# One order of 2925 operations replaced by another in a fused recurrence and MLP kernel

## The chip, the cores and the metric

The kernel runs on one core of a Trainium2 chip. The metric is the time of one execution on the device in microseconds (us); less is better. The engines are named PE (TensorE, the matrix engine, with its weight loads as PEld), DVE (VectorE), ACT (ScalarE), POOL (GpSimd) and SP, whose queue issues nearly all transfers. Each engine works through its own instructions in order; semaphores hold one until what it needs from another engine or a transfer is there.

## The reference

For 4 x 8 heads, 768 steps and head width 40, a recurrence on a 40 x 40 state reads `y = r . state`, decays the state by `w`, subtracts the product of `state . a` with `b` and adds that of `v` with `k`. All heads' `y`, laid side by side to 320 numbers per token (3072 tokens), go through a gated MLP without a nonlinearity. `moe_w1` to `moe_w_out` come as 64-bit floats, the rest as 32-bit.

```python
def _attn_ref(r, k, v, w, a, b):
    for t in range(S):
        y[:, :, t] = np.einsum('bhd,bhde->bhe', rt, state)
        Sa = np.einsum('bhde,bhe->bhd', state, at)
        state_decay = state * wt[:, :, None, :] - np.einsum('bhd,bhe->bhde', Sa, bt)
        state = state_decay + np.einsum('bhd,bhe->bhde', vt, kt)
...
def _moe_ref(x, w1, w2, w3, w_out):
    a = x @ w1
    b = x @ w2
    h = a * b @ w3
    return (h @ w_out).astype(np.float32)
```

## The kernel before

**Stages.** The 768 steps are cut into 12 chunks of 64. For each chunk, the four batches are taken in two pairs. A pair is loaded (`load`: ld.fm, ld.xx, ld.aa), scaled by the running product of `w` (`scale`: sc.max, sc.scan, sc.ln, sc.exp, sc.aa, sc.gt, sc.gi, sc.xs), and multiplied into the triangular blocks of the chunk (`causal`: ca.mm and its copies and masks). `solve` inverts these blocks on DVE (so.in, then some 35 small operations so.x, so.td, so.tt), and `join` puts the parts together on PE. `pairs` and `tokens` (pa, tk) prepare further operands. `rec` then applies them for the two batches of a pair at a time: r.zv, r.s, r.zn, r.t0, r.t1, r.t2, r.tr, all matmuls of line 870; between r.t0 and r.t1, and between r.t1 and r.t2, DVE makes one masked product `un` each (r.u, line 921). With two pairs in a chunk there are 24 in all. `gather` moves the results of a chunk by twelve small transfers (ga, line 946), and `mlp` runs the MLP of the chunk: m.xh and m.xl split the input in two, m.mm1 are the wide matmuls (line 987), m.a, m.ab, m.gh and m.gl their results, m.mm2 (line 1012) the second product, m.o and m.out the output.

**Weights.** Ahead of all this, `weights` reads the 31 blocks of 64-bit weights (cv.in, 512 KB each) into four buffers `raw` and makes 32-bit numbers of them (cv.t and cv.add on DVE, cv.r on ACT, cv.sign on either), and `product` multiplies the last two weight matrices on PE (w3.mm, line 539). The MLP can't begin before this is done (the last `nil`). At the end `proof` reads the blocks a second time (ck.in) and checks their range (ck.abs, ck.sq, ck.max).

**The order.** Every operation is declared by `op` with its kind, what it reads and what it writes. `Order.place` (line 300) sorts all of them by `RANK[kind][n]`, where n counts the operations of a kind in the order of their declaration; the ranks are a permutation of 0 to 2924. It hands out buffers in that order (`SLOTS`, line 35: 4 raw, 3 xx, 3 aa, 4 fm, 8 banks of PSUM, one y and one xr), emits the instructions in it, and ties every instruction to the one before it on its engine. So RANK fixes the order on each engine and in SP's queue, and semaphores do the rest:

```python
placed, done = sorted(self.ops, key=lambda o: RANK[o["kind"]][o["i"]]), set()
```

**The choice of engine.** Seven kinds can run on two engines. `ON[kind]` has a letter for each of their operations: d for DVE, p for POOL, a for ACT (`both`). A POOL operation that shares its port with DVE is made to wait for the DVE operation of two inputs that stands last before it in the order (line 1143 on).

Of the kernel before, what the change touches and what calls it, by code (L numbers as in the profile page):

```python
# [55 lines left out]
    "cv.sign": "dddadaaaddddaaaadaaaaaaddaaaaaa",  # L56
    "cv.add": "dddddddddddddddddddppdpdpdpdddd",
    "w.lo": "ddppdpdddddp",
    "sc.aa": "ddddddddpdpppppppdppddpd",
    "sc.xs": "ddddddpppdddddpdddpdpdpd",  # L60
    "m.gl": "dddpdpddpppppppppdpppppdddpppppddppdpppdpddddddp",
    "ck.sq": "dddaaddadaaaaadddadaaaddaadadda",
}
RANK = {kind: [int(n) for n in ranks.split()] for kind, ranks in {
# [1198 lines left out]
```

## Time and profile before

| | before |
|---|---|
| runs, us | 604.8, 596.65, 604.96 |
| median of the runs, us | 604.8 |
| profiled execution, us | 607.17 |
| its span, first to last instruction, us | 605.5 |
| mean granted clock of PE, share of full speed | 0.976 |
| instructions | 26713 |

The profile is of one execution with a time of its own, 607.17 us, of which its 605.5 us of span are recorded; busy times, waits and clocks are of that execution, while the median is over the runs. Busy shares are means over stages with different limits. A wait is put down to the semaphore that came last; "issue" is idle time for which the profile shows no releaser.

### The profile page before, as it was taken

Reading aid. Unit: us, or ns where it says so; the run is one execution under the profiler, and the core shown is the slowest. Engines: PE = TensorE matmul, PEld = TensorE weight load, DVE = VectorE, ACT = ScalarE, POOL = GpSimd, SP = SyncE. Lnnn points to the kernel's source line nnn. Section 1 sums busy time; section 2 is a strip of 40 time slices with the busy share of each in tenths; the row PEclk is TensorE's granted clock in tenths of the full one; section 3 lists DMA queues with packets and bytes.
Section 4 is the critical chain, followed back from the end, with each engine's and each line's share of the span. In section 5 each row is a group of like instructions: output and inputs, shape, how many; then the busy total and the mean of one; then the engine's idle time right before and its main releaser. Section 6 shows DMA issues by size and latency. Waiting matters only on the chain.

```text
span 605.5 us, 26713 instructions
## 1 busy us (share of the span) xinstructions
PE 546.8 (90%) x11714; PEld 490.9 (81%) x11714; DVE 494.3 (82%) x950; ACT 414.2 (68%) x889; POOL 156.3 (26%) x222
## 2 busy tenths in 40 slices
PE   1298988899999799999999899998999999999994
PEld 1276666799988799898898799898898989988994
DVE  6999879999599777795797797995998978956663
ACT  6878949855847647648756649649578488477762
POOL 3012332122412312244323223044141142031000
PEclk9997989899999979999999999999999999999998
DMA  8997875350244335223353343532665343255681
GB/s 254 308 289 232 267 202 162 72 160 15 75 114 117 83 91 139 64 68 99 100 127 109 90 116 104 136 85 64 162 168 146 105 129 110 93 157 180 210 253 59
DMA packets 56812, 83.45 MB, mean 138 GB/s; under 512 B 30320, under 2 KB 38000, under 8 KB 56688
## 3 DMA queue, kind: packets, MB, share of 16 engines
q1 hardware_dynamic: 56300, 81.34, 47.4%
q8 instruction: 94, 1.54, 1.1%
q10 hardware_dynamic: 388, 0.33, 0.2%
q14 instruction: 30, 0.25, 0.1%
HBM read 72.99 MB, written 3.93 MB: 127 GB/s over the span
## 4 chain that ended last, share of the span: by engine, by line
PE 47%; DVE 17%; ACT 16%; DMA 8%; issue 5%; SPq 4%; POOL 1%; ACTq 0%; DVEq 0%; POOLq 0%
PE bank L987 19%; PE bank L870 12%; PE bank L1012 5%; ACT JP L329 4%; ACT TT L329 4%; PE bank L539 3%; SPq L946 3%; DVE tmp L680 3%; PE bank L628 2%; PE bank L845 2%; DMA raw<-in_wo_dram 2%; DMA raw<-in_w3t_dram 2%; PE bank L821 1%; DVE TDX L656 1%; DVE un L921 1%
## 5 line engine op out<-in xcount | busy, mean ns | idle before, releaser
L987 PE MATMUL bank<-xs,W 128*128 128x256 f32 x1536 | 209.0, 288 | 0.0
L987 PEld LDWEIGHTS bank<-xs,W 128*128 128x128 f32 x1536 | 190.1, 191 | 7.3 <-issue 0.8
L830 POOL TENSOR_SCALAR_AFFINE_SELECT vg<-vg 64x256 f32<-64x256 f32 x96 | 40.3, 426 | 145.9 <-DVE tmp L680 72.2
L1003 POOL TENSOR_TENSOR gl<-ga,gh 128x512 fp32r<-128x512 f32 x28 | 36.1, 1290 | 121.7 <-DVE tmp L680 46.1
L1012 PE MATMUL bank<-W3h,gh 128*128 128x320 f32 x192 | 62.3, 324 | 0.2
L1012 PE MATMUL bank<-W3h,gl 128*128 128x320 f32 x192 | 59.6, 310 | 0.9 <-POOL gl L1003 0.5
L1012 PE MATMUL bank<-W3l,gh 128*128 128x320 f32 x192 | 59.2, 309 | 0.0
L870 PE MATMUL bank<-un,bk 64*40 64x104 f32 (+1 forms) x768 | 44.8, 255 | 10.0 <-DVE un L921 7.8
L644 POOL TENSOR_SCALAR_AFFINE_SELECT lm<-lm 64x512 f32<-64x512 f32 x48 | 33.5, 699 | 76.2 <-DVE tmp L680 25.4
L329 ACT ACTIVATE JP<-bank 64x256 f32<-64x256 f32 (+2 forms) x120 | 45.2, 378 | 10.8 <-PE bank L628 8.3
L329 ACT ACTIVATE ga<-bank 128x512 f32<-128x512 f32 x48 | 28.6, 598 | 30.8 <-PE bank L987 30.5
L870 PE MATMUL bank<-hs,TT 64*64 64x104 f32 x768 | 46.6, 260 | 2.2 <-ACT TT L329 1.7
L329 ACT ACTIVATE gh<-ga 128x512 fp32r<-128x512 f32 x48 | 30.2, 631 | 25.5 <-DVE ga L1000 24.2
L870 PEld LDWEIGHTS bank<-un,bk 64*40 64x40 f32 (+1 forms) x768 | 35.7, 124 | 13.6 <-DVE un L921 11.2
L921 DVE TENSOR_TENSOR un<-bank,mask_h 128x416 f32<-128x416 f32 x48 | 28.1, 584 | 22.7 <-PE bank L870 22.6
L870 PE MATMUL bank<-vg,bk 64*40 64x104 f32 (+1 forms) x768 | 45.0, 255 | 0.3 <-issue 0.2
L1000 DVE TENSOR_TENSOR ga<-bank,ga 128x512 f32<-128x512 f32 x48 | 32.8, 686 | 13.1 <-ACT ga L329 7.2
L870 PEld LDWEIGHTS bank<-hs,TT 64*64 64x64 f32 x768 | 36.7, 136 | 7.5 <-ACT TT L329 3.0
L539 PE MATMUL bank<-wof,w3f 128*128 128x320 f32 x128 | 42.7, 488 | 0.0
L628 PE MATMUL bank<-aa,xx 40*64 40x64 f32 x1536 | 30.5, 232 | 12.9 <-DVE xx L600 5.5
L628 PEld LDWEIGHTS bank<-aa,xx 40*64 40x64 f32 x1536 | 27.4, 145 | 17.3 <-issue 8.7
L680 DVE TENSOR_TENSOR tmp<-Tp,TDX 128x256 f32<-128x256 f32 (+2 forms) x57 | 39.9, 700 | 1.0
(126 smaller groups left out, 1265.5 us busy)
## 6 DMA issues: line engine op xcount, KB each, us to landing
rv<-in_rv_dram SPq DMA_DIRECT2D x24, 588.0 KB
xx<-in_fmx_dram SPq DMA_DIRECT2D x24, 448.0 KB
raw<-in_w3t_dram SPq DMA_DIRECT2D x16, 512.0 KB
JP<-in_w3t_dram SPq DMA_DIRECT2D x11, 512.0 KB
fm<-in_fmg_dram SPq DMA_DIRECT2D x24, 227.5 KB
aa<-in_fma_dram SPq DMA_DIRECT2D x24, 224.0 KB
raw<-in_w_dram SPq DMA_DIRECT2D x10, 512.0 KB
vg<-in_vt_dram SPq DMA_DIRECT2D x48, 80.0 KB
```

What stands on the lines that cost most here:

```text
L329: act.activation(out_, in_, AF.Copy, scale=scale)
L539: pe.matmul(out=pt.t[:, 0:DM], lhsT=w[:, j], rhs=wof[:, j], start=(j == 0), stop=(j == NJ - 1))
L628: pe.matmul(out=bank(s)[64 * z:64 * z + 64, i, p], lhsT=X[r, p, z], rhs=aa.t[r, i, p], start=True, stop=True)
L644: op("ca.mask", lambda q=q: pool.affine_select(out=lm.t[q], in_=lm.t[q], pattern=[[0, 2 * NP], [1, C]], compare_op=ALU.is_gt, fill=0.0, ba ...
L680: dve.tensor_tensor(out=scratch(*shape), in0=x().to_broadcast([128, *shape]), in1=y().to_broadcast([128, *shape]), op=ALU.mult)
L830: op("pa.mask", lambda q=q, vg=vg: pool.affine_select(out=vg.t[q, :, 0:C], in_=vg.t[q, :, 0:C], pattern=[[0, NP], [1, C]], compare_op=ALU. ...
L870: pe.matmul(out=out_(ab ^ z, p), lhsT=left(ab, ab ^ x, p), rhs=right(ab ^ x, p), start=start and p == 0, stop=True, skip_group_check=True)
L921: dve.tensor_tensor(out=un[i].t, in0=view(hp[i]), in1=mask_h.unsqueeze(1).to_broadcast([128, NP, N]), op=ALU.mult)
L987: pe.matmul(out=pt.t[:, TOK * x:TOK * x + TOK], lhsT=WT[k][:, cs], rhs=xs.t[:, z], start=(n == 0), stop=(n == 7))
L1000: op("m.ab", lambda a=a, pt=pt: dve.tensor_tensor(out=a.t, in0=wide(pt), in1=a.t, op=ALU.mult), r=[pt], w=[a])
L1003: both("m.gl", lambda e, a=a, j=j: e.tensor_tensor(out=gl.t[:, j:j + 2], in0=a.t, in1=gh.t[:, j:j + 2], op=ALU.subtract), r=[a, (gh, j)], ...
L1012: pe.matmul(out=pt.t[:, 0:DM], lhsT=l.t[:, j, ts], rhs=W3[r][:, j], start=(j == 0 and n == 0), stop=(j == NJ - 1 and n == 2))
```

## The change

The two tables ON and RANK get other numbers. Each kind has as many operations as before, no instruction's shape or count changes but for the engine that runs it, and the rest of the file is the same. All 79 kinds have other ranks. In ON, cv.sign has 22 letters a instead of 20 (of 31), cv.add 5 p as before at other places, w.lo 3 p instead of 4, sc.aa 9 instead of 11, sc.xs 4 instead of 7, m.gl 30 instead of 28 (and its last letter is d instead of p), and ck.sq 13 a instead of 16. The order is described as made anew for the same structure, with later landings assumed for the first transfers. Of the diff, all of ON and the kinds that are spoken of:

```diff
--- before.py
+++ after.py
@@ -53,199 +53,200 @@
 ON = {
-    "cv.sign": "dddadaaaddddaaaadaaaaaaddaaaaaa",
-    "cv.add": "dddddddddddddddddddppdpdpdpdddd",
-    "w.lo": "ddppdpdddddp",
-    "sc.aa": "ddddddddpdpppppppdppddpd",
-    "sc.xs": "ddddddpppdddddpdddpdpdpd",
-    "m.gl": "dddpdpddpppppppppdpppppdddpppppddppdpppdpddddddp",
-    "ck.sq": "dddaaddadaaaaadddadaaaddaadadda",
+    "cv.sign": "aadaaddaadadaaaaddaaaaaadaadaaa",
+    "cv.add": "dddddddpdddddddddddpdpddddpdpdd",
+    "w.lo": "dddpddpddddp",
+    "sc.aa": "ddddddddpdpppddppdpdpdpd",
+    "sc.xs": "ddddddpddddddppdddpddddd",
+    "m.gl": "ddddppppppdpdpdpdpppddpppdpdpppdpppdpppppppdddpd",
+    "ck.sq": "ddaaaaaaddddaddadddaadaadddddda",
 }
...
-    "z.bk": "10 13 22 24 26 28 32 37",
+    "z.bk": "2 4 7 9 11 14 26 28",
...
-    "sc.max": "29 8 63 136 417 470 563 687 820 889 1059 1141 1238 1355 1437 1551 1694 1746 1905 2005 2120 2219 2350 "
-            "2469",
+    "sc.max": "25 16 64 182 419 459 569 700 823 888 1085 1144 1221 1317 1435 1533 1689 1783 1889 1976 2142 2247 2368 "
+            "2476",
...
-    "sc.scan": "31 12 67 150 429 473 567 724 827 898 1067 1146 1252 1370 1439 1599 1703 1810 1914 2023 2132 2243 2364 "
-            "2486",
+    "sc.scan": "29 17 66 192 426 465 581 720 831 896 1100 1148 1230 1367 1437 1591 1698 1798 1896 2006 2151 2253 2402 "
+            "2479",
...
-    "sc.ln": "35 18 74 160 435 484 583 733 833 905 1071 1156 1266 1400 1444 1604 1709 1822 1918 2028 2150 2255 2368 "
-            "2491",
+    "sc.ln": "37 18 72 199 435 479 600 732 844 907 1106 1156 1241 1396 1442 1599 1703 1804 1907 2012 2166 2258 2411 "
+            "2494",
...
-    "sc.exp": "52 21 82 177 440 487 599 737 838 908 1076 1159 1271 1406 1447 1608 1714 1828 1922 2031 2169 2259 2422 "
+    "sc.exp": "39 20 81 201 446 485 634 736 850 909 1114 1159 1262 1398 1445 1601 1710 1810 1909 2014 2219 2264 2434 "
             "2498",
...
-    "cv.in": "2 49 227 159 9 20 61 77 81 41 6 5 89 114 133 121 214 198 167 317 246 268 265 179 218 243 306 364 337 455 "
-            "352",
+    "cv.in": "5 33 213 172 8 44 54 68 74 55 10 12 97 110 85 120 220 162 152 290 248 260 268 191 205 245 317 362 360 "
+            "382 365",
...
-    "cv.r": "16 78 259 196 45 66 108 104 127 69 48 33 163 149 188 165 237 223 209 347 312 322 331 225 244 300 363 428 "
-            "385 526 404",
+    "cv.r": "22 65 255 214 32 69 78 105 112 86 45 49 144 160 137 173 263 203 178 340 311 323 335 221 241 287 352 393 "
+            "411 519 405",
...
-    "ld.fm": "3 0 14 84 372 419 544 618 797 851 1039 1107 1215 1321 1424 1506 1673 1725 1881 1988 2098 2198 2309 2421",
+    "ld.fm": "6 0 35 122 380 432 544 657 806 857 1050 1093 1205 1291 1420 1481 1670 1727 1873 1962 2121 2191 2319 2429",
...
-    "ld.xx": "11 4 51 200 349 407 556 586 569 888 1042 1099 999 1349 1410 1549 1473 1716 1737 1958 2128 2224 2162 2402",
+    "ld.xx": "15 3 58 194 385 406 541 612 582 890 927 1066 1243 1288 1391 1511 1558 1711 1688 1994 2220 2199 2042 2359",
...
-    "ld.aa": "7 1 54 137 345 443 571 721 803 916 1029 1139 1221 1385 1435 1581 1676 1806 1888 2033 2216 2230 2452 2348",
+    "ld.aa": "13 1 57 163 388 471 537 714 815 910 1030 1134 1229 1388 1431 1563 1681 1806 1883 2022 2130 2232 2468 "
+            "2471",
...
-    "so.in": "101 284 581 779 979 1205 1458 1640 1863 2078 2308 2540",
+    "so.in": "106 283 568 782 979 1203 1461 1640 1872 2078 2308 2533",
...
-    "m.xh": "559 682 917 1176 1361 1567 1795 2008 2269 2489 2673 2832",
+    "m.xh": "559 676 934 1177 1340 1573 1788 2018 2276 2492 2672 2832",
...
-    "r.t0": "313 357 502 551 754 808 988 1032 1171 1241 1399 1440 1631 1670 1842 1898 2062 2112 2271 2353 2494 2576 "
-            "2730 2762",
+    "r.t0": "313 372 501 545 758 800 985 1033 1167 1233 1397 1439 1624 1668 1834 1900 2068 2125 2273 2357 2495 2564 "
+            "2736 2767",
...
-    "r.t1": "335 382 515 561 767 817 1000 1047 1178 1258 1408 1448 1637 1686 1851 1915 2071 2130 2278 2375 2522 2585 "
-            "2740 2772",
+    "r.t1": "326 383 510 557 769 818 998 1055 1182 1247 1406 1452 1636 1686 1853 1913 2075 2140 2285 2371 2521 2577 "
+            "2747 2774",
...
-    "r.t2": "351 399 528 573 780 828 1013 1065 1194 1277 1414 1461 1648 1702 1864 1927 2080 2143 2293 2381 2545 2595 "
-            "2775 2778",
+    "r.t2": "347 397 524 565 784 830 1026 1068 1191 1253 1411 1462 1649 1696 1860 1926 2096 2152 2298 2380 2535 2597 "
+            "2764 2784",
...
```

## Rows read from the trace of the kernel before

**Rows 1.** The page, part 1: busy us (share of the span) and instructions of an engine.

```profile
PE 546.8 (90%) x11714; PEld 490.9 (81%) x11714; DVE 494.3 (82%) x950; ACT 414.2 (68%) x889; POOL 156.3 (26%) x222
```

**Rows 2.** Windows: stretch, its length, busy us, granted clock, DMA share, GB/s.

```profile
0.00:30.00 30.00, 6.25 (x153) 5.42 (x157) 24.57 (x41) 22.93 (x47) 5.75 (x24) 1.00 0.96 281
30.00:120.00 90.00, 80.03 (x1729) 59.50 (x1725) 81.33 (x165) 74.32 (x153) 22.84 (x33) 0.92 0.70 203
120.00:590.00 470.00, 453.26 (x9811) 419.38 (x9804) 382.71 (x733) 312.68 (x684) 126.45 (x165) 0.99 0.43 119
590.00:605.50 15.50, 7.23 (x49) 6.60 (x47) 5.67 (x13) 4.28 (x8) 1.29 (x1) 0.85 0.21 61
```

**Rows 3.** Waits of PE: us in total, times, longest us.

```profile
PE bank L870 <- DVE un L921: 7.8, 10, 1.5
PE bank L870 <- issue: 7.0, 7, 2.1
```

**Rows 4.** Windows around three idle times of PE that have no releaser.

```profile
82.60:84.50 1.90, 0.01 (x1) 0.00 (x0) 1.87 (x3) 1.90 (x6) 0.65 (x1) 1.00 0.96 304
84.50:90.00 5.50, 5.50 (x53) 3.85 (x56) 2.12 (x3) 0.34 (x2) 1.65 (x2) 0.69 0.44 121
...
209.90:212.00 2.10, 0.00 (x0) 0.00 (x0) 2.00 (x6) 0.00 (x0) 0.75 (x1) 0.91 0.64 228
212.00:219.00 7.00, 6.99 (x99) 6.01 (x103) 3.80 (x10) 1.45 (x3) 1.51 (x4) 0.54 0.46 112
...
540.60:541.85 1.25, 0.04 (x3) 0.00 (x0) 0.58 (x1) 1.16 (x3) 0.00 (x0) 1.00 0.83 197
541.85:546.00 4.15, 4.15 (x35) 3.77 (x38) 0.81 (x3) 1.22 (x3) 0.00 (x0) 0.61 0.99 333
```

**Rows 5.** Timeline, 0 to 60 us: start, us, engine, line, idle before and releaser.

```profile
4.20 0.72 ACT L573 ACTIVATE gt<-fm,limit 104x512 f32<-104x512 f32 x1 [2.10 <-POOL stats L371]
...
5.04 0.95 ACT L329 ACTIVATE bank<-ident 32x416 f32<-32x416 f32 x2
...
5.12 1.22 DVE L578 TENSOR_TENSOR_SCAN fm<-fm,first 104x520 f32<-104x520 f32 x1
...
7.36 0.78 ACT L457 ACTIVATE rs<-raw 128x512 uint16<-128x512 uint16 x1 [1.37 <-DMA raw<-in_w_dram]
...
8.01 0.60 ACT L582 ACTIVATE gi<-fm 104x512 f32<-104x512 f32 x1
...
10.85 1.22 DVE L600 TENSOR_TENSOR xx<-xx,gi 104x1024 f32<-104x1024 f32 x1
```

**Rows 6.** Waits of DVE: us in total, times, longest us.

```profile
DVE aa L589 <- DMA aa<-in_fma_dram: 2.0, 2, 1.2
```

**Rows 7.** Windows of ten us in the middle.

```profile
330.00:340.00 10.00, 7.36 (x273) 6.38 (x271) 6.41 (x7) 9.16 (x21) 3.63 (x6) 1.00 0.08 13
340.00:350.00 10.00, 9.74 (x284) 8.61 (x284) 9.59 (x29) 4.18 (x12) 1.30 (x1) 1.00 0.46 126
```

**Rows 8.** Groups by line and form: count, busy us, mean ns, idle time before.

```profile
L600 DVE TENSOR_TENSOR xx<-xx,gi 104x1024 f32<-104x1024 f32 x17 | 20.8, 1221 | 0.4
L600 POOL TENSOR_TENSOR xx<-xx,gi 104x1024 f32<-104x1024 f32 x7 | 17.0, 2433 | 8.0 <-issue 4.8 <-DVE gi L596 2.8 <-DVE tmp L680 0.4
...
L589 DVE TENSOR_TENSOR aa<-aa,fm 104x512 f32<-104x512 f32 x13 | 9.2, 711 | 2.0 <-DMA aa<-in_fma_dram 2.0
```

**Rows 9.** Timeline, 575 us to the end.

```profile
594.50 1.29 POOL L1003 TENSOR_TENSOR gl<-ga,gh 128x512 fp32r<-128x512 f32 x1 [34.91 <-DVE JP L491]
...
595.84 0.42 PE L1012 MATMUL bank<-W3h,gl 128*128 128x320 f32 x1 [0.53 <-POOL gl L1003]
```

**Rows 10.** Waits of SP, and two rows of the timelines of SP and ACT.

```profile
SPq L443 <- DVE w3f L446: 20.0, 9, 5.2
...
80.38 0.33 SPq L561 DMA_DIRECT2D fm<-in_fmg_dram  x1
...
92.56 0.71 ACT L573 ACTIVATE gt<-fm,limit 104x512 f32<-104x512 f32 x1
```

316 rows, old and new, of the table RANK are left out of this document.

## The prediction, made before the changed kernel was run

> **What bounds the kernel now.** I read the page's busy times first. TensorE (PE) is busy 546.8 of 605.5 us and DVE 494.3 [rows 1], so neither is full over the whole. The table by stretches comes second, because a mean over stages hides the limit of each. From 120 to 590 us PE is busy 453.26 of 470 us: there PE is the bound and only 16.7 us are idle. In the first 30 us it works 6.25 us and DVE 24.57; from 30 to 120 us PE works 80.03 and DVE 81.33 of 90 [rows 2]. So before the first MLP matmul the vector engine, fed by loads, sets the pace, and afterwards PE does. Adding the four stretches, PE is idle 58.7 us (605.5 less 546.8): 33.7 before 120, 16.7 in the long middle, 8.3 at the end. No reordering can give back more than these plus what PE loses at the lower clock.
>
> Third, the waits of PE: ten waits of line 870 for `un` (DVE, the masked product between r.t0, r.t1 and r.t2) make 7.8 us, and seven that the view calls "issue" make 7.0 [rows 3]. Three of the latter are long: 82.6 to 84.5, 209.9 to 212.0 and 540.6 to 541.85. In each, PE does next to nothing, and right behind it the granted clock is 0.69, 0.54 and 0.61 [rows 4], a mixture of the two levels, 1.2 and 2.4 GHz.
>
> Fourth, the timeline of the first microseconds [rows 5]: it shows what each engine stood before when data came late.
>
> **The change part by part.** No instruction is new and none is gone: all 2925 operations have a counterpart. Only their order on each engine (RANK) and the engine of some (ON) change. So the sum goes over waits.
>
> *The head.* Before, ACT is free 2.10 us ahead of 4.20, where the first sc.max runs [rows 5]; scan runs from 5.12 to 6.34; the logarithm that needs it starts only at 8.01, because ACT stands in order and cv.r of the first weight block is ahead of it, waiting until 7.36 for its landing. So 8.01 less 6.34 = 1.67 us are lost behind a landing. After, six of the eight z.bk (ranks 2 to 14) come first: two take 0.95 us, six 2.85, from 2.10 to 4.95, so sc.max starts 0.75 us later; but sc.ln (18) and sc.exp (20) stand ahead of cv.r (22). Net 1.67 less 0.75 = 0.9 us earlier for xx, whose multiply runs at 10.85 now. DVE's own longest wait for landings, that for aa, is 2.0 us in all [rows 6], so even a perfect guess of the landings gives DVE no more than that and the 0.9. I take 1 us off; bounds 0 (PE is not the limit here, and DVE's next blocks may land no sooner) and 3.
>
> *Up to the first MLP matmul.* Sorting the DVE operations by rank up to the first m.mm1 (rank 566 before, 571 after) gives the same set but for swaps: three cv.add for three others, six cv.sign less and four more, one w.lo less and two more, and the transpose so.in of the third chunk, now ahead (rank 568). PE has the fourth r.t2 (rank 565) ahead of it now, and one group of transposes less. What is pulled ahead is not to be done later, so I take 0; bounds 2 us either way, about one such transpose.
>
> *The waits for un.* For each of the 24 pairs (numbered from 0) I took the PE operations ranked between r.t0 and r.t1, and between r.t1 and r.t2. Before, five places have none at all (r.t0 to r.t1 of pairs 3, 8, 12, 16, 18, as ranks 2062 and 2071 for pair 16), two more have only a small transpose or product of pa. After, two have none (pair 0 between r.t0 and r.t1, ranks 313 and 326; pair 14 between r.t1 and r.t2, ranks 1853 and 1860) and two have something small: seven thin places become four. Ten waits cost 7.8 us [rows 3], 0.78 each; three fewer give 2.3. Bounds: 0, if DVE's own queue ahead of r.u sets the wait, and 7.8, if all go. These waits leave the clock alone: from 330 to 340 us PE is idle 2.64 of 10 us, the most of any ten in the middle, and the granted clock is 1.00 there and in the next ten [rows 7]. The Trainium skill ("TensorE: Matmul & The Clock Gate", section "HAM oscillation — how this bites in real kernels") says that idle gaps between bursts of matmuls drop the clock, and that the warm-up is paid again after each. By that rule each wait removed would also return the 1.7 us lost behind the first stall, and the sum would be 5.1 us better; the rows just named speak against it here.
>
> *The choices of engine.* To DVE come three sc.xs, two sc.aa and one w.lo from POOL and three ck.sq from ACT; from it go two m.gl to POOL and two cv.sign to ACT. One sc.xs is 1.22 us on DVE (2.43 on POOL); I let the sc.aa row, 0.71, stand for the other kinds [rows 8]. DVE gets 3 x 1.22 + 2 x 0.71 = 5.1 us more (six to it and four from it leave two of the smaller). From 120 to 590 us DVE has 87 us free [rows 2], which hides it: 0. If that cover is gone, because the additions fall just ahead of an r.u, it costs up to 5.1.
>
> *The end.* The last m.gl runs on POOL from 594.50 for 1.29 us, and PE waits 0.53 us for it [rows 9]. After, the last letter of m.gl is d: DVE's half as long form takes the wait away, 0.5 us off. Bounds 0 and 0.53.
>
> *The issue stalls.* Nothing in the trace releases them and nothing in the diff names them. They cost 1.89 + 2.10 + 1.21 = 5.2 us of idleness, and the low clock behind costs 0.31 x 5.5 + 0.46 x 7.0 + 0.39 x 4.15 = 6.5 us: 11.7 in all [rows 4]. I keep them: 0; bounds 11.7 off (all gone) and, for two more of the mean size, 7.8 on.
>
> Sum: 1 + 0 + 2.3 + 0 + 0.5 = 3.8 us off the profiled execution's 607.17, that is 603.4. That execution lies 2.4 us over the median of the runs shown, 604.8; on the scale of that median the forecast is 601.0.
>
> **The rivals.**
>
> *The stalls go.* They lie inside line 870's products, and DMA moved 304, 228 and 197 GB/s during them [rows 4], more than the 119 of the middle [rows 2]. A new order puts other loads beside other products. All three gone gives 601.0 less 11.7 = 589.3; the two dearest gone (1.89 + 1.7 and 2.10 + 3.2 = 8.9) gives 592. For it: one of the runs shown took 596.65 without any change. Against: the loads are as many as before. 0.2.
>
> *The order does not bring what it says.* The waits for un were made by DVE's queue, not by thin cover; the 0.9 us of the head is swallowed by DVE's work. Then 605 to 607 as before. For it: the DVE sums up to the first MLP matmul are alike. 0.23.
>
> *The weight loads hold back the second chunk's.* Before, the last raw block (cv.in 29) stands at rank 455, behind the second chunk's loads; now four raw loads (ranks 360, 362, 365, 382) stand around fm at 380 and ahead of xx at 385 and aa at 388. SP issues in order, and each raw load waits for its buffer; such a wait lasts up to 5.2 us. fm was issued at 80.38 and sc.max used it at 92.56 [rows 10]: 12.2 us of slack. Four waits of 5.2 make 20.8; what exceeds 12.2, 8.6 us, holds ACT's queue, with SB and un copies behind it, and PE for these. That gives 601.0 + 8.6 = 609.6, slower than before. It decides from 12.2 us on. Against: the buffers these four need are let go at ranks 331 to 368, ahead of them. 0.1, and passing 2% would take four waits of 7 us.
>
> **How the numbers follow.** The forecast, a small gain, has 0.47; the other three 0.2, 0.23, 0.1. The time is the forecast's 601.0. The range goes down to 589 (all stalls gone) and up to 614 (the slower rival with half of the DVE additions uncovered, 609.6 + 2.6, and 2 us of the first stage); what lies outside is under 2 in 10. The forecast's own range is 594 to 607: 601 less the 5.5 us more that all un waits and the 1 us more that the head could give, and 601 with none of the 3.8 us and 2 us of the first stage on top. Two per cent of 604.8 is 12.1 us, about what a measurement of this kernel can tell from no change. Faster by more needs under 592.7: nearly all of the stalls rival, 0.18. Slower by more needs over 616.9: 0.04 from the last rival, and 0.04 for a wait in a place that these rows don't show. Within: 0.74.
>
> **What would show it.** In the profile of the changed kernel: sc.ln right behind scan, and the multiply of xx near 10 us; PE's waits for un near 5.5 us in some seven waits; no wait of PE for POOL's gl at the end; DVE near 499 us; PE busy at least 453 of 470 us in the middle; the first MLP matmul (line 987) near 120 us. Wrong it would be if line 987 began many microseconds later, if stalls named issue were more or fewer than three long ones, or if PE waited for DVE in new places.

## The result, and the profile after

The changed kernel takes 599.21 us in the median (22 runs, 594.07 to 604.0), the kernel before beside it 604.86 (22 runs): a ratio of 0.9911, 95% interval 0.9882 to 0.9940. Run a second time beside other runs of the kernel before it took 599.89 against 605.64, 0.9907 (0.9868 to 0.9947). The forecast was 601.0, a change within 2%. The medians differ by 5.65 us, where the sum had 3.8.

The profiled execution took 603.52 us, its span is 601.8: 3.7 less than before. That this is within 0.1 of the sum is luck of the two executions: this one is the third slowest of the 22 runs, and a second profile of each kernel (below) has spans of 603.5 and 596.5, 7.0 apart. Part 1 of the page of the changed kernel answers to [rows 1], the windows to [rows 2] (stretch, length, busy us of PE, PEld, DVE, ACT, POOL with instructions, granted clock, DMA share, GB/s):

```profile
PE 544.7 (91%) x11714; PEld 491.4 (82%) x11714; DVE 496.2 (82%) x955; ACT 411.9 (68%) x888; POOL 149.1 (25%) x218
```

```profile
0.00:30.00 30.00, 5.71 (x136) 4.89 (x136) 22.87 (x38) 23.72 (x46) 5.30 (x23) 1.00 0.95 272
30.00:120.00 90.00, 79.76 (x1776) 60.55 (x1780) 82.03 (x168) 75.54 (x156) 23.61 (x32) 0.92 0.73 211
120.00:590.00 470.00, 454.99 (x9786) 422.02 (x9776) 389.90 (x746) 311.65 (x686) 120.20 (x163) 0.99 0.43 119
590.00:601.80 11.80, 4.20 (x30) 3.90 (x29) 1.42 (x6) 1.00 (x3) 0.00 (x0) 0.76 0.14 35
```

The first 120 us are no shorter: PE did 85.5 us of work in them, before 86.3, and the first matmul of the MLP starts at 120.5, before at 120.6. In the long middle PE is idle 15.0 us instead of 16.7, and the last stretch is 3.7 us shorter (as both are cut at 590 us, that is the whole difference of the spans). The waits of PE in the changed kernel (us in total, times, longest) against [rows 3]:

```profile
PE bank L846 <- DVE xx L601: 18.3, 2, 11.2
PE bank L629 <- DVE aa L590: 7.3, 2, 6.9
PE bank L871 <- DVE un L922: 5.5, 9, 1.1
PE bank L755 <- issue: 3.1, 1, 3.1
...
PE bank L629 <- ACT xs L972: 1.7, 2, 1.0
PE bank L783 <- DVE TDX L734: 1.7, 4, 0.9
...
PE bank L1013 <- POOL gl L1004: 0.6, 1, 0.6
```

The waits for `un` made by DVE fell from 7.8 to 5.5 us. The waits for the `un` that ACT writes, of which the kernel before has this row, are not in the table any more. New ones came: `xs` 1.7 us, and `TDX` from 0.5 to 1.7.

```profile
PE bank L870 <- ACT un L329: 2.7, 4, 1.0
```

The end of the timeline (start, us, engine, line, operation) answers to [rows 9]:

```profile
593.77 0.31 PE L1013 MATMUL bank<-W3h,gl 128*128 128x320 f32 x1
594.01 0.19 PE L1175 MATMUL bank<-good,ones 128*1 128x1 f32 x2
```

The last product of the proof follows the last m.mm2 with no wait. Before, PE stood 0.53 us for POOL's `gl` and then 0.82 us for ACT's `o` ahead of this product; both are gone. The rows of the second wait, in the kernel before:

```profile
597.26 0.31 PE L1012 MATMUL bank<-W3h,gl 128*128 128x320 f32 x1
598.39 0.19 PE L1174 MATMUL bank<-good,ones 128*1 128x1 f32 x2 [0.82 <-ACT o L329]
```

This second wait did not set the end. From the end of the last m.mm2 matmul to that of the span there are 7.9 us before and 7.7 after (second profiles 7.9 and 7.6), for ACT still copies the last `o` behind that matmul, at 597.90 before and at 594.41 after.

### The profile page after: what moved, and what is told of

The parts are those of the page before. It is cut to its first block, busy times and chain, and to the rows that moved or that the text cites. A ratio compares the mean times of both kernels' runs of the same rounds, so it can differ in the third digit from the quotient of the medians.

```text
span 601.8 us, 26711 instructions
## 1 busy us (share of the span) xinstructions
PE 544.7 (91%) x11714; PEld 491.4 (82%) x11714; DVE 496.2 (82%) x955; ACT 411.9 (68%) x888; POOL 149.1 (25%) x218
## 3 DMA queue, kind: packets, MB, share of 16 engines
q8 instruction: 94, 1.54, 1.1%
## 4 chain that ended last, share of the span: by engine, by line
PE 56%; DVE 21%; ACT 12%; issue 5%; DMA 4%; SPq 1%; ACTq 0%; POOL 0%; DVEq 0%
PE bank L988 24%; PE bank L871 15%; PE bank L1013 9%; DVE tmp L681 4%; ACT JP L330 3%; PE bank L629 3%; ACT TT L330 2%; DVE TDX L657 2%; PE bank L846 2%; DMA fm<-in_fmg_dram 2%; PE bank L822 1%; PE bank L783 1%; DVE Tp L685 1%; DVE un L922 1%; DVE TDX L685 1%
## 5 line engine op out<-in xcount | busy, mean ns | idle before, releaser
L1004 POOL TENSOR_TENSOR gl<-ga,gh 128x512 fp32r<-128x512 f32 x30 | 38.6, 1288 | 145.1 <-DVE tmp L681 49.8
L831 POOL TENSOR_SCALAR_AFFINE_SELECT vg<-vg 64x256 f32<-64x256 f32 x96 | 42.4, 448 | 117.8 <-DVE tmp L681 48.5
L871 PE MATMUL bank<-un,bk 64*64 64x104 f32 (+1 forms) x768 | 46.2, 258 | 5.6 <-DVE un L922 5.5
L871 PEld LDWEIGHTS bank<-un,bk 64*64 64x64 f32 (+1 forms) x768 | 36.4, 126 | 12.3 <-DVE un L922 8.5
L846 PE MATMUL bank<-ident,xx 104*128 104x104 f32 x192 | 27.4, 273 | 18.3 <-DVE xx L601 18.3
L629 PE MATMUL bank<-aa,xx 40*64 40x64 f32 x1536 | 32.2, 237 | 10.5 <-DVE aa L590 7.3
L540 PE MATMUL bank<-wof,w3f 128*128 128x320 f32 x128 | 40.6, 471 | 0.0
L629 PEld LDWEIGHTS bank<-aa,xx 40*64 40x64 f32 x1536 | 29.1, 150 | 14.0 <-issue 10.5
```

The costliest lines, as they stand in the source:

```text
L540: pe.matmul(out=pt.t[:, 0:DM], lhsT=w[:, j], rhs=wof[:, j], start=(j == 0), stop=(j == NJ - 1))
L629: pe.matmul(out=bank(s)[64 * z:64 * z + 64, i, p], lhsT=X[r, p, z], rhs=aa.t[r, i, p], start=True, stop=True)
L831: op("pa.mask", lambda q=q, vg=vg: pool.affine_select(out=vg.t[q, :, 0:C], in_=vg.t[q, :, 0:C], pattern=[[0, NP], [1, C]], compare_op=ALU. ...
L846: pe.transpose(out=bank()[:, p], in_=X[:, p].rearrange("q x t -> q (x t)"), identity=ident[0:104, 0:104])
L871: pe.matmul(out=out_(ab ^ z, p), lhsT=left(ab, ab ^ x, p), rhs=right(ab ^ x, p), start=start and p == 0, stop=True, skip_group_check=True)
L1004: both("m.gl", lambda e, a=a, j=j: e.tensor_tensor(out=gl.t[:, j:j + 2], in0=a.t, in1=gh.t[:, j:j + 2], op=ALU.subtract), r=[a, (gh, j)], ...
```

## The experiments

The order of a kernel is its RANK table, the choice of engines its ON table; nothing else is edited. Theory one is that of the sum: the new order gives TensorE other work to do between the matmuls of a recurrence step, the choices of engine bring nothing by themselves. Its rivals are named with the runs.

**How far two profiles of one kernel agree.** The same two kernels again.

```diff
 (no line differs from the changed kernel)
```

> The changed kernel once more, instruction by instruction the same, for how far two profiles of one kernel agree. 598 to 601 us, ratio 0.988 to 0.994. If the waits are a property of the order: waits of TensorE for un within 0.5 us of the 5.5 of the first profile, at the same places. If the stalls with no releaser and the stretches at half clock are a property of the order too: a stall of 1.3 us near 411 us and half clock near 412 and 456 us again; if they are a property of the execution, they lie elsewhere.

599.89 us, ratio 0.9907 (0.9868 to 0.9947); this profile's span is 596.5. Waits for `un` from DVE: 5.1 us in eight, at the places of the first profile. The stall at 411 us is there too (1.18 us), but not the half clock behind it. Windows of 5 us of the changed kernel's first profile, then of its second; the clock is the last column but two:

```profile
410.90:415.90 5.00, 4.92 (x109) 4.66 (x113) 0.53 (x1) 2.73 (x6) 0.97 (x2) 0.66 0.45 135
455.00:460.00 5.00, 4.23 (x102) 4.01 (x103) 3.73 (x6) 4.41 (x12) 2.26 (x4) 0.66 0.33 90
```

```profile
410.90:415.90 5.00, 4.16 (x132) 3.78 (x136) 0.69 (x1) 4.15 (x10) 0.80 (x2) 1.00 0.42 129
455.00:460.00 5.00, 5.00 (x156) 4.44 (x149) 4.04 (x9) 4.36 (x10) 2.28 (x4) 1.00 0.21 41
```

So the waits, and the stall at 411 us, go with the order; these two stretches at half clock (1.2 of 2.4 GHz) go with the execution. Each lasts 3.4 us in the record of the clock, half of which is lost: 3.4 of the 5.3 us between the two spans.

```diff
 (no line differs from the kernel before)
```

> The kernel before once more, for how far two profiles of it agree. 600 to 608 us. If the waits belong to the order: waits for un within 0.5 us of 7.8 in ten, and stretched VectorE operations within 1 us of the 4.6 of the first profile; if the half-clock stretches belong to the execution: they lie elsewhere than near 212 and 543 us.

604.68 us; beside 25 runs of the same kernel with a median of 602.21 this is a ratio of 1.007 (1.0029 to 1.0110). Nothing differs, so one such interval is too narrow by about 0.7%, and differences below that from one set of runs alone are not shown here. The gain of 0.9% is not far above it, but both sets of runs of the changed kernel have it. The clock doesn't make it: over the runs its mean is 0.9831 and 0.9826 in the changed kernel, 0.9805, 0.9827, 0.9832 and 0.9844 in the kernel before, and by the slope given at the end of this document a difference of 0.002 goes with 1.2 us. The waits for `un` from DVE are 9.0 us in twelve, 1.2 more than in the first profile (0.5 was expected), and half clock lay at 211.9 us again, at 543 not.

**One part of the order alone.** Rival: the gain comes from the start, where the landings were re-assumed.

```diff
 (the 559 operations ahead of the first MLP matmul: new order and engines; the rest as before)
-    "sc.ln": "35 18 74 160 435 484 583 733 ...
+    "sc.ln": "37 18 72 199 435 479 584 733 ...
```

> The new order and engines for the 559 operations ahead of the first MLP (weights, first chunk, most of the second), the old ones for all behind it. Theory (the gain of 5.6 us comes from the long middle, where the vector engine is waited for in fewer places; the first stage is set by the amount of DVE work and gives nothing): 604 to 606 us, ratio 1.00, with the first MLP matmul near 120.5 us. Rival (the gain comes from the start, that is from the later landings that the order was made for): 599 to 600 us, ratio 0.991, whatever the order behind.

609.47 us, 1.0113 (1.0074 to 1.0152). The waits for `un`, from DVE and ACT together, are 10.6 us in 14, as in the kernel before (10.5 in 14), and the first MLP matmul starts at 121.7 us. The start brings no gain; why the time is longer than before isn't shown.

```diff
 (old order and engines up to the first MLP; the rest new; four operations put off for their buffers)
-    "m.mm1": "619 639 614 633 582 585 566 592 ...
+    "m.mm1": "626 639 634 644 606 613 578 599 ...
```

> The reverse: the old order up to the first MLP, the new one behind it (four operations stand a few places later, so that the buffers suffice). Theory: 599 to 600 us, ratio near 0.991. Rival (the start): 604 to 606 us, ratio 1.00. If both halves give half, each lies near 602.

604.89 us, 1.0010 (0.9969 to 1.0052). The waits for `un` are 5.3 us in ten, as in the changed kernel (5.8 in ten). But the first MLP matmul starts at 128.5 us and the other waits are 11.7 us (8.4 before). From that matmul to the end this profile takes 479.4 us, the changed kernel's two profiles 481.3 and 476.5, those of the kernel before 484.9 and 482.2. So the few waits for `un` come with the new order of the middle, and so does a gain there; 8 us are lost ahead of it. Part of these is the clock (20.5 us at half clock up to there, before 13.7 and 6.8); why the cut costs the rest isn't shown. The rival of the start fails. As far as one profile shows, theory one is borne out for the stretch behind the first MLP matmul; it fails for the whole time once the order is cut in two.

**Cover added by hand.** If a thin place costs 0.78 us and nothing else changes, filling it must help.

```diff
 (old order; five TensorE operations moved ahead, so that four more places have cover)
-    "ca.mm": "68 43 103 239 482 564 751 763 906 933 1165 1182 ...
+    "ca.mm": "68 43 103 239 482 561 751 763 906 933 1165 1178 ...
```

> The old order with five PE operations moved forward by a few places, so that four of its seven thin places (pairs 3, 5, 8 and 18) have about a microsecond of other matmuls while DVE makes un; one more, between r.t1 and r.t2 of pair 5, keeps what it had. Theory (a thin place costs 0.78 us of PE): PE's wait for un falls from 7.8 to about 4.7 us, 3 us less, 602 us, ratio 0.995. Rival (the waits for un only change places, and the moved operations are missed elsewhere): un falls, but the time stays at 605, ratio 1.00.

610.56 us, 1.0111 (1.0065 to 1.0157). Waits of PE in this kernel (other line numbers: 765 is 870, 523 is 628 of before), and the row of its timeline for one of the moved operations:

```profile
PE bank L765 <- DVE un L816: 4.7, 6, 1.5
...
PE bank L523 <- POOL aa L484: 2.3, 2, 1.9
PE bank L523 <- ACT xs L866: 2.2, 2, 2.0
```

```profile
244.58 1.16 PE L523 MATMUL bank<-aa,xx 40*64 40x64 f32 x64 [1.90 <-POOL aa L484]
```

The waits of this line for `un` did fall, from 7.8 to 4.7 us. But the moved operations were not ready: this ca.mm stands where the kernel before waits 1.10 us for `un`, and waits 1.90 us for POOL's `aa` itself; another waits 1.99 us for ACT. The clock added to it. Windows of this kernel just behind that wait and 2 us behind a later one of 1.29 us, then of the kernel before at about the same work:

```profile
246.00:249.40 3.40, 3.40 (x48) 2.93 (x42) 0.59 (x1) 2.79 (x6) 2.18 (x4) 0.51 0.12 32
328.00:331.40 3.40, 3.40 (x24) 3.17 (x27) 2.12 (x3) 2.00 (x5) 2.72 (x4) 0.50 0.85 261
```

```profile
245.00:248.40 3.40, 3.40 (x131) 3.20 (x125) 1.42 (x4) 2.97 (x7) 2.71 (x5) 1.00 0.26 54
325.40:328.80 3.40, 3.40 (x87) 3.22 (x87) 2.10 (x3) 2.75 (x7) 2.40 (x3) 1.00 0.87 253
```

```diff
 (new order; fifteen TensorE operations moved ahead, so that each place has 1.5 us of cover)
-    "r.t1": "326 383 510 557 769 818 998 1055 1182 ... 1636 1686 1853 1913 2075 ...
+    "r.t1": "326 383 510 557 769 818 998 1055 1183 ... 1636 1686 1853 1913 2076 ...
```

> The new order with fifteen PE operations moved forward, so that from the third chunk on most places between r.t0, r.t1 and r.t2 have 1.5 us or more of other matmuls. Theory: the 3.1 us that PE waits for un behind 120 us fall to about 1, 597 us, ratio to before 0.987. Rival (what is left there is not set by thin cover): 599 us, ratio 0.991 as the new order; worse, if the moved MLP matmuls now wait themselves.

606.95 us, 1.0059 (1.0026 to 1.0092). The waits for `un` did not fall (6.7 us in eleven), and new ones came: POOL's `gl` 2.4 us, `y` 1.5, `ga` 1.2. Here cover beyond what the order has only moved waits to other operations. The first MLP matmul starts 3 us later than in the changed kernel, at 123.6, with a stall of 4.5 us ahead of it for which the profile shows no releaser.

```diff
 (new order; in pairs 4 to 23 r.u, r.t1, r.u, r.t2 right behind r.t0)
-    "r.t1": "326 383 510 557 769 818 998 1055 1182 ...
+    "r.t1": "326 383 510 557 760 802 987 1039 1169 ...
```

> The changed kernel, but in all pairs but the first four the tensor matmuls of a step and the evictions to un between them stand back to back, so that nearly all of 40 places have no other TensorE work in them. If a wait for un is paid in full by the path that sets the end (0.78 us a place, as worked out ahead of the result): 40 x 0.78 = 31 us more, 630 us, and waits for un of over 30 us in the trace. If a place left open is mostly won back because the chain behind it comes earlier: under 612 us, with the waits for un in the trace all the same.

641.37 us, 1.0614 (1.0559 to 1.0669). A row of the waits, and one place in the timeline:

```profile
PE bank L871 <- DVE un L922: 30.0, 40, 1.1
```

```profile
301.62 0.26 PE L871 MATMUL bank<-hs,TT 64*64 64x104 f32 x2
302.64 0.30 PE L871 MATMUL bank<-un,bk 64*64 64x104 f32 x2 [0.76 <-DVE un L922]
```

Forty waits of 0.75 us each: the price of an open place, read as 0.78 ahead of the result, was right, and nearly none of it is won back. The whole is dearer: matmuls of such a group start 0.09 us apart, here 1.02 lie between two, so a place costs 0.93 us, of which 0.76 is recorded as waiting and the rest counts as busy. 40 x 0.93 = 37 us, of which the changed kernel has part already (5.5 us of these waits); PE also waits some 6 us longer for ACT's `un`, `hs` and `lm` and for POOL's `gl`. The span is 37.9 us longer than that of the changed kernel's first profile and 43.2 longer than that of the second, and the medians differ by 41.5.

**Order and choices apart.**

```diff
 (new RANK; ON as in the kernel before, for instance)
-    "sc.xs": "ddddddpddddddppdddpddddd",
+    "sc.xs": "ddddddpppdddddpdddpdpdpd",
-    "ck.sq": "ddaaaaaaddddaddadddaadaadddddda",
+    "ck.sq": "dddaaddadaaaaadddadaaaddaadadda",
```

> The new order of all operations, each on the engine it had in the kernel before. Theory one (the order brings the gain, the choices between engines bring nothing by themselves): 598 to 602 us, ratio to before 0.988 to 0.995. Rival (an order is ranked for the engines it was planned with, so that with the old choices an operation stands behind others on a busy engine): the gain is gone, 603 to 607, ratio 0.998 to 1.005, and PE waits more for un or TDX than in the changed kernel.

619.98 us, 1.0223 (1.0190 to 1.0256).

```diff
 (old RANK; ON as in the changed kernel, for instance)
-    "sc.xs": "ddddddpppdddddpdddpdpdpd",
+    "sc.xs": "ddddddpddddddppdddpddddd",
```

> The old order of all operations with the new choices between engines. Theory one (the choices bring nothing by themselves): 602 to 606 us, ratio 0.998 to 1.003; VectorE near 496 us busy, hidden. Rival (the gain comes from the choices): 598 to 601, ratio 0.99 to 0.995. A third answer, over 606, would say that order and choices belong together.

623.36 us, 1.0304 (1.0264 to 1.0345). Neither half of the change brings anything: the order alone costs 14.3 us, the choices alone 17.7, both together gain 5.7. The third answer, that they belong together, is the one that holds, and with it theory one's second half falls. Of the losses some 6 and 10 us lie ahead of the first MLP matmul, which starts at 126.8 and 130.3. The waits of PE, summed from the view of each kernel by what was awaited (`un` from DVE and ACT; "others" without the first loads' `xx`, `aa`, `rs`, `bk` and without "issue"):

| kernel | `un`, us (times) | others, us |
|---|---|---|
| before, two profiles | 10.5 (14), 12.4 (16) | 8.4, 9.3 |
| changed, two profiles | 5.8 (10), 5.4 (9) | 9.8, 7.7 |
| new order, old choices | 7.7 (10) | 17.7 |
| old order, new choices | 15.3 (20) | 17.2 |

With the new order there are nine or ten waits for `un` under either choices, with the old one 14 to 20; choices that the order was not ranked for double the rest. One way in which they do is to be seen on DVE. Rows of DVE, then of POOL, in the new order with the old choices:

```profile
191.13 2.91 DVE L681 TENSOR_TENSOR tmp<-Tp,TDX 128x1024 f32<-128x1024 f32 x1
193.96 1.23 DVE L579 TENSOR_TENSOR_SCAN fm<-fm,first 104x520 f32<-104x520 f32 x1
...
463.15 2.80 DVE L579 TENSOR_TENSOR_SCAN fm<-fm,first 104x520 f32<-104x520 f32 x1 [0.82 <-ACT gt L574]
```

```profile
190.57 2.38 POOL L601 TENSOR_TENSOR xx<-xx,gi 104x1024 f32<-104x1024 f32 x1 [4.08 <-DVE gl L1004]
...
462.46 2.39 POOL L601 TENSOR_TENSOR xx<-xx,gi 104x1024 f32<-104x1024 f32 x1 [3.19 <-DVE gl L1004]
```

The scan takes 1.23 us at 193.96 and 2.80 at 463.15, where it starts 0.7 us behind a multiply of POOL and ends 1.10 us behind that one's end (462.46 + 2.39 = 464.85). The product at 191.13 ends 1.09 us behind POOL's end. Both these operations of DVE read two tiles in SBUF (on-chip memory; `bank` names PSUM, where the products of PE land), and both stand until POOL is done. The Trainium skill ("SBUF — State Buffer", section "Who interferes with whom") calls the pair of ports that the two share an exclusive lock: who starts first holds it for its whole instruction, the other blocks. These rows agree. Not every DVE operation is held: `un`, which reads a bank of PSUM and one tile in SBUF, takes its usual 0.58 us in the changed kernel beside a multiply of POOL that has 2.1 us to run:

```profile
297.08 0.58 DVE L922 TENSOR_TENSOR un<-bank,mask_h 128x416 f32<-128x416 f32 x1
...
296.80 2.39 POOL L601 TENSOR_TENSOR xx<-xx,gi 104x1024 f32<-104x1024 f32 x1 [8.90 <-PE bank L822]
```

So POOL delays `un` through held operations ahead of it on DVE, not at `un` itself. Such stretching, taken over the median time of a form in these profiles for all DVE operations that ran at least 0.15 us over it, is 4.3 and 3.9 us in the two profiles of before, 2.6 and 2.8 in those of the changed kernel, 14.7 in the new order with the old choices (the expectations below go by 17.3) and 9.3 in the old order with the new ones; nearly all of these have a POOL operation beside them. The kernel's own guard ties a POOL operation to the DVE operation ahead of it, not to the one behind; that one the order has to keep away, if both its inputs lie in SBUF.

**Which of the choices.** Theory two: stretching makes the loss, so the choices between DVE and POOL matter. Rival: any choice that the order was not ranked for costs alike, 0.32 us.

```diff
 (new order; m.gl, sc.xs, sc.aa, w.lo, cv.add as in the kernel before, for instance)
-    "w.lo": "dddpddpddddp",
+    "w.lo": "ddppdpdddddp",
```

> The new order; of the choices between engines only those between VectorE and GpSimd are the old ones (38 operations: 21 go to GpSimd, 17 to VectorE), those between VectorE and ScalarE are the new ones. Theory two (in an order ranked for other engines, a GpSimd operation comes to lie beside VectorE operations, which then last until it ends; the new order with all old choices had 17.3 us of such stretching on VectorE, the changed kernel 2.7): most of the loss of the new order with the old choices stays, 612 to 620 us, and VectorE operations stretched by 10 us or more. Rival (any choice that the order was not ranked for costs alike, the 20 us of all 63 shared out, 0.32 us each): 600 + 38 x 0.32 = 612 us. A rival on the other side (the loss is ScalarE's evictions, put behind squares and signs that now lie there): 600 to 604 us.

614.21 us, 1.0135 (1.0047 to 1.0223); stretching 15.2 us. Few waits for `un` are not enough: behind the first MLP matmul this profile has 1.8 us of them in four, the changed kernel 3.4 in seven, but PE's other waits there are 9.8 us instead of 6.5.

```diff
 (new order; ck.sq and cv.sign as in the kernel before, for instance)
-    "ck.sq": "ddaaaaaaddddaddadddaadaadddddda",
+    "ck.sq": "dddaaddadaaaaadddadaaaddaadadda",
```

> The new order; of the choices between engines only those between VectorE and ScalarE are the old ones (25 operations), those between VectorE and GpSimd are the new ones. Theory two: little is lost, 600 to 606 us, VectorE operations stretched by less than 5 us. Rival (0.32 us for each choice): 600 + 25 x 0.32 = 608 us. The rival on the other side (it is ScalarE): 612 to 620 us.

606.68 us, 1.0044 (0.9993 to 1.0096); stretching 4.6 us. A row of the timeline, of a wait where the changed kernel waits 0.71 us:

```profile
377.08 0.42 PE L871 MATMUL bank<-un,bk 64*64 64x104 f32 x2 [2.21 <-DVE un L922]
```

```diff
 (new order and choices, but the 17 operations that only the new choices have on POOL are on DVE, for instance)
-    "w.lo": "dddpddpddddp",
+    "w.lo": "dddpdddddddp",
```

> The new order and the new choices, but the 17 operations that only the new choices have on GpSimd run on VectorE, so GpSimd has less to do and VectorE some 12 us more (17 times 0.68 to 1.22 us). Theory two: VectorE stays unstretched (under 3 us), and the 12 us are mostly hidden, 600 to 606 us; what is lost is evictions to un that stand behind a moved operation, up to 0.7 us each. Rival (a wrong engine costs by where the operation then stands, and stretching has no part in it): as much for each as in the kernel with the old choices between VectorE and GpSimd, 17/38 of its loss.

604.42 us, 1.0029 (0.9989 to 1.0069); DVE busy 504.5 us, stretching 2.9. Theory two expected 612 to 620, 600 to 606 and 600 to 606; the rival's numbers are 612, 608 and, with 17/38 of the measured 14.3 us, 606.3. Both fit within 2.2 us, so these runs don't tell them apart. They do show that the choices between DVE and POOL carry most of the loss (by the ratios, 2.3 of the 3.2% that all old choices cost under the new order), that they bring the stretching with them, and that stretching isn't all: without it, 17 more operations on DVE lose the gain too, as far as a difference this small can be read. In the last profile this loss lies ahead of the first MLP matmul, which starts at 124.0 us with 20.5 us at half clock ahead of it (changed kernel 13.7); from there to the end it takes 478.4 us, like the changed kernel (481.3 and 476.5).

## Why the prediction was right, point by point

- *The head.* Right as a mechanism, of little or no gain. The rows of the changed kernel that answer to [rows 5]:

```profile
2.10 2.71 ACT L330 ACTIVATE bank<-ident 32x416 f32<-32x416 f32 x6
4.84 0.72 ACT L574 ACTIVATE gt<-fm,limit 104x512 f32<-104x512 f32 x1
5.68 1.24 DVE L579 TENSOR_TENSOR_SCAN fm<-fm,first 104x520 f32<-104x520 f32 x1 [0.50 <-ACT gt L574]
6.96 0.63 ACT L583 ACTIVATE gi<-fm 104x512 f32<-104x512 f32 x1 [1.31 <-DVE fm L579]
9.78 0.78 ACT L458 ACTIVATE rs<-raw 128x512 uint16<-128x512 uint16 x1 [1.44 <-DMA raw<-in_w_dram]
9.83 1.23 DVE L601 TENSOR_TENSOR xx<-xx,gi 104x1024 f32<-104x1024 f32 x1
```

  The logarithm follows the scan, and `xx` is multiplied at 9.83 instead of 10.85. Over all profiles the new head starts it at 9.82 or 9.83 whether that conversion starts at 9.07 or at 10.48; with the old head it starts at 10.85, 10.97, 11.15, 11.97 and 12.65 for conversions at 7.36, 7.48, 7.65, 8.47 and 8.54. So the new head no longer depends on the first landing. But PE's next wait, 6.88 us for `aa` ahead of 20.88, ends only 0.62 us earlier than the one of 5.50 us before it, and the first MLP matmul starts at 120.5 (second profile 120.0; before 120.6 and 121.2). I took 1 us off; the first profiles show 0.1, the second ones 1.2 for all that lies ahead of it.
- *Up to the first MLP matmul.* 0 taken; nothing beyond these 0.1 and 1.2 us was measured.
- *The waits for un.* The right mechanism, but the term was too small. 2.3 us were taken and 2.3 measured in the first profiles (7.8 to 5.5), with nine waits, not seven; in the second ones it was 3.9 (9.0 to 5.1, twelve waits to eight), so the exact match is luck. The price of a place was right to 0.03 us as a wait, and is 0.93 from matmul to matmul. Left out of the sum were the waits for the `un` from ACT, 2.7 and 3.4 us in the two profiles of before and none after.
- *The choices of engine.* 0 taken, and as a term of its own this was the wrong step, although the number came out: priced alone they cost 17.7 us. I asked whether DVE had room, not what stands where the operations go. DVE's busy time grew by 1.9 us instead of 5.1; it has 1.1 to 1.7 us less stretching.
- *The end.* 0.5 us taken; the wait for `gl`, 0.53 us (0.80 in the second profile), is gone, but not for the reason given. In the new order with the old choices the last m.gl runs on POOL, and PE has no wait for it; in the old order with the new choices PE waits for POOL near the end all the same. A row of the timeline of the one, then one of the waits of the other:

```profile
608.37 1.29 POOL L1004 TENSOR_TENSOR gl<-ga,gh 128x512 fp32r<-128x512 f32 x1 [35.61 <-ACT gh L330]
```

```profile
PE bank L1013 <- POOL gl L1004: 1.7, 1, 1.7
```

  So the order took the wait away and not the letter d. The wait for `o` I had not counted, and it did not set the end.
- *New waits*, not in the sum: `xs`, `TDX`, `vg` and `ga`, 4.6 us together where they were 0.8 (3.9 in the second profile); one of 0.55 us for POOL's `gl` at 568 us.
- *The issue stalls.* 0 taken: 7.6 us against 8.0, in the second profiles 7.5 against 8.5. The longest, 3.10 us at 55.57, has a counterpart of 1.46 us at 55.0 in the second profile of before. Where they can come is fixed in PE's own instruction stream (last section). The rival that had them all gone fell, and so did the one with the weight loads: the first MLP matmul was not late. The rival by which the order brings nothing fell with the ratio of 0.9911.
- *The signs of being wrong.* Two of them came: PE waits for DVE in new places (`TDX`), and of the stalls without a releaser two, not three, are over 1 us (3.10 and 1.27).

So the sum came out near by terms that cancel: the waits for `un` gave more than was taken, and new waits that it hadn't took part of that back. From the first MLP matmul to the end, where nearly all of the difference lies, the two profiles of each kernel are made up of (us):

| | before | changed |
|---|---|---|
| PE's waits for `un`, from DVE and ACT (times) | 7.7 (10), 8.5 (11) | 3.4 (7), 2.9 (6) |
| its stalls without a releaser | 5.8, 4.5 | 4.5, 4.8 |
| its other waits and short gaps | 4.6, 4.6 | 7.1, 5.3 |
| PE busy | 459.9, 457.8 | 458.7, 456.1 |
| behind the last matmul | 6.9, 6.8 | 7.6, 7.5 |
| all | 484.9, 482.2 | 481.3, 476.5 |

The waits for `un` fell by 4.3 and 5.6 us; other waits took back 2.5 and 0.7. PE's busy time fell by 1.2 and 1.7 us, as less of it ran at half clock (6.8 us and none, before 10.2 and 6.8), and that belongs to the execution.

The rule weighed in the prediction, that idle gaps bring the clock down (the Trainium skill, "TensorE: Matmul & The Clock Gate", section "HAM oscillation — how this bites in real kernels"), would have made the gain 5.1 us larger. By the two profiles of each kernel the clock gave nothing back for sure: the stretches at 412 and 456 us came and went with no change of the kernel. Half clock did follow three waits of 1.90, 1.29 and 2.21 us above, but neither the one of 1.99 us at 117.9 in the kernel with cover added to the old order nor the one of 1.54 us at 340 in the kernel before. So the length of a wait did not decide it here.

## What to carry over

An order and the choice of engines that it was ranked for are one thing: cut in two, mixed, or mended by hand each of the ten variants here was slower than the whole, by the ratios 1 to 7%. So price a choice of engine by what stands beside and behind the operation in that order, above all whether a GpSimd operation comes to lie beside a VectorE one with both inputs in SBUF, and not by whether the engine has room. And look up every group of waits for the same tile, whichever engine writes it, before summing what an order may save.

## What was not expected of the hardware

- A DVE operation with both inputs in SBUF took up to 2.91 us instead of 1.23 beside one of POOL and ended 1.1 us behind POOL's end; `un`, with one input in PSUM, took its usual time.
- The stalls of PE for which the profile shows no releaser keep to places in PE's own instruction stream. If all records of its queue are counted (matmuls, weight loads, semaphores), 69 of the 70 such stalls of 0.5 us or more in the 14 profiles stand 194 or 195 records behind a multiple of 256. A kernel has some 92 of these places, and three to seven of them stall in an execution; some come again (1.27 and 1.18 us at 411 us, 3.10 and 2.73 at 55 us in the changed kernel, 2.11 and 1.84 at 212 us before), others don't. What happens at such a place, and why some stall, stays open; no run here tried it.
- The same stall of 1.2 us was followed by half clock in one execution (0.66 in the next 5 us) and by the full clock in another (1.00). Over the 36 runs of the kernel before beside the first four experiments, 0.01 of the mean granted clock goes with 6.1 us of time, with a correlation of -0.77: more than half of the variance of one kernel's times (595.91 to 611.35) goes with the clock.
- The record of the clock begins at 37.6 us in the kernel before, so the 1.00 that the windows show for the first 30 us is no measurement: 64 matmuls of line 628 take 1.99 us at 21.50, and as many of the same shape 1.16 us at 244.58 in the kernel with cover added to the old order (row above).
